# DeltaNet and hash-routed experts on one core: third expert's rows ahead of its weights, and other filler products in a planned order

## Chip, cores and metric

The kernel runs on one core of one Trainium2 chip. The metric is the device time of one execution in microseconds (us), given as the median of several runs. Everything is float32.

## What is computed

The reference has two stages. First, for 4 batches x 8 heads, a recurrence over 768 steps with a 48 x 48 state; then a mixture of 8 experts over the 3072 resulting rows of 384 numbers, where each row goes to exactly one expert, chosen by a hash of its token number.

```python
k_n = k / (norm(k) + 1e-6)
for t in range(S):                      # S = 768, D = 48, B = 4, H = 8
    y[:, :, t] = q[t] @ state
    v_old = state . k_n[t]
    state = state + beta[t] * outer(k_n[t], v[t] - v_old)
x = y.transpose(0, 2, 1, 3).reshape(B * S, H * D)       # 3072 x 384
expert_idx = token_ids * 2654435761 % 8
for e in range(8):
    xe = x[expert_idx == e]
    out[expert_idx == e] = relu(xe @ w1[e]) @ w2[e]      # 384 -> 1024 -> 384
```

## The kernel before

**Recurrence.** Time is cut into 24 chunks of 32 steps, and four chunks make a group. Per group the keys and queries are loaded (SP queue), turned on the tensor engine PE (`turn`, L457) and copied from PSUM to the tile KQ or wide by the scalar engine ACT (L462). Products of keys with keys and with queries follow: `first_gram` (L525) for the first group, `gram` (L483) for the others; ACT and the vector engine DVE copy them out as GK and GQ (L493, L500, L503, L509, and L537, L538 for the first group). `inverse` (L581 to L624) inverts a 32 x 32 triangular matrix per chunk and head on DVE in pairs of operations, a multiply into tmp (L624) and an add into U (L622); `turn_back` (L638) transposes it for PE.

Each chunk then is a chain across engines: PE multiplies the state with keys (L690, L659 into psX) and queries (L659 into psY), ACT makes the residual R (L695), PE solves with the inverse (L709), ACT copies W (L723), PE updates the state (L738 into psS) and finishes the answer (L779 into psY), ACT copies the new state S (L762) and the rows x_sb (L788), and GpSimd (POOL) scatters the rows, sorted by expert, into a DRAM scratch (L794).

**The order is planned, not written.** Every step of that stage is recorded by `task` with an engine, an assumed duration and what it reads and writes. `order` (L286) plays a greedy schedule of these tasks when the program is built and emits each engine's instructions in the planned order; on the chip each engine runs its own list strictly in that order. While it plans, `fill` (L320) looks at each planned idle stretch of PE in front of a task. If the stretch is over FILL_OVER (380 ns) and begins before FILL_UNTIL, it puts products of the identity matrix (emitted at L1192) in front of that task, of 128 to 512 columns each, into a PSUM bank that the plan holds to be unused. Nobody reads these products. How much idle time of one stretch may be filled is capped: at 1100 ns, except in the first 2 us. Each filler also counts two instruction words (`issued += 2`). The planner assumes that instructions are fetched in blocks of 256 words and lets PE's tasks wait for them, so another number of words also shifts planned start times and with them the order of later tasks.

**Experts.** RANKS orders the eight experts as 4, 0, 1, 2, 3, 5, 6, 7. The first is computed inside the planned stage: its products (L1041, L1052, and for the rows of the last chunks L1065 and L1075) are low-priority tasks that take PE's idle time. Its late hidden values, h_late, lie in the row buffer xq0, and L1075 is what reads them last. The other seven come after it as plain code. For each, `gemm1` (L1226) makes 8 hidden blocks of three products each in four PSUM banks in turn; ACT applies the relu to the even blocks (L1229), DVE to the odd ones (L1231). Then comes the second product (L1263, turned back by L1273 and copied by L1248; or L1242), and POOL scatters the rows to the output (L1252). Inside `gemm1` the function `between` starts what later experts need: after block 0 the weights of an expert further on, after block 1 the row fetch of the expert after the next, and after blocks 1, 3 and 5 DVE turns one third of the next expert's rows (L108), in DVE's own list ahead of its later relus.

All these loads are on one queue, SP's, which issues in program order and stops at a load whose buffer isn't free:

- `fetch` (L100, L104): four row loads into xq0 or xq1 and one small load of token numbers. Second, fourth, ... expert by rank use xq1; the third uses xq0.
- `load_w` (L94 four loads of 384 KB, L117 one of 1536 KB): an expert's weights.

At the start of the part that follows the planned stage, L1303 to L1307 issue: rows of the second expert, its weights (`parts`, eight loads at L94 and L125), weights of the third expert, rows of the third expert.

```python
            fetch(RANKS[1])                                                             # 1303
            for part in parts:
                part()
            w_tiles[2] = load_w(expert_at(RANKS[2], mybir.EngineType.SP), w_pool2, nc.sync)
            fetch(RANKS[2])                                                             # 1307
```

Of the kernel before, what the change touches and what calls it, by code (L numbers as in the profile page):

```python
# [20 lines left out]
def kernel(  # L21
# [27 lines left out]
    RANKS = [4, 0, 1, 2, 3, 5, 6, 7]  # L49
# [35 lines left out]
    def value(at, engine, top):  # L85
        return nc.values_load(ov_i[0:1, at:at + 1], engines=[engine], min_val=0, max_val=top)

    def expert_at(rank, engine):
        return value(AT_E + rank, engine, E - 1)

    def w1_parts(e, w1_sb, eng):

        w1 = moe_w1[bass.ds(e, 1)].rearrange("o d f -> (o d) f")
        return [lambda j=j: eng.dma_start(  # L94
            out=w1_sb[C * j:C * j + C],
            in_=w1[QD * j:QD * j + QD].rearrange("(c d) f -> d c f", d=C)) for j in range(4)]

    def load_x(row, blocks, xq, eng):
        rows = x_dram[bass.ds(row, C * blocks)].rearrange("(i t) x -> t i x", t=C)
        return [eng.dma_start(out=xq[C * j:C * j + C, 0:blocks, 0:QD],  # L100
                              in_=rows[:, :, QW * j:QW * j + QD]) for j in range(4)]

    def load_numbers(row, cols, width, to, eng):
        return eng.dma_start(out=to, in_=x_dram[bass.ds(row, cols * width), QD:QD + 1].rearrange(  # L104
            "(c p) x -> p c x", c=cols))
# [5 lines left out]
    def load_w(e, pool, eng):  # L111
        s2 = moe_w2[bass.ds(e, 1)].rearrange("o f d -> (o f) d")
        w1_sb = pool.tile([P, CO, F], F32, name="w1_sb")
        for part in w1_parts(e, w1_sb, eng):
            part()
        w2_sb = pool.tile([P, FO, DIN], F32, name="w2_sb")
        eng.dma_start(out=w2_sb, in_=s2.rearrange("(fo p) d -> p fo d", p=P))  # L117
        return w1_sb, w2_sb
# [40 lines left out]
    with ExitStack() as phase1:  # L159
# [9 lines left out]
        BANK = 512  # L169
        LATE = NU - GC  # L170
        SEED, SPREAD, PATIENCE = 1, 0.0, 0.2
        FILL_OVER, FILL_UNTIL = 380.0, 80000.0

        st = phase1.enter_context(tc.tile_pool(name="st", bufs=1))
        iv_stack = ExitStack()
# [110 lines left out]
        def order():  # L286
# [33 lines left out]
            def fill(i, idle, at):  # L320

                nonlocal issued
                rate = 1.67
                if at < 2000:

                    rate, idle = 3.34, idle - 900
                idle = min(idle, 2750 if at < 2000 else 1100)
                while idle > FILL_OVER and at < FILL_UNTIL:
                    unused = [b for b in range(len(homes)) if banks[b] is not None
                              and banks[b] <= at]  # L330
                    if not unused:
                        break
                    n = min(4, max(1, int((idle - 160) / (rate * P))))
                    fills.setdefault(i, []).append((unused[0], n))
                    issued += 2
                    idle -= n * rate * P
                    at += n * rate * P
# [17 lines left out]
            while len(done) < n:  # L355
                best, can = None, {}
                for e, r in ready.items():
                    can[e] = [(x, i) for x, i in ((when(x, i), i) for x, i in r)
                              if x is not None]
                    if can[e]:  # L360
                        at = max(free[e], min(x for x, _ in can[e]))
                        if best is None or at < best[0]:
                            best = (at, e)
                at, e = best
# [27 lines left out]
                if e == "PE":  # L392
                    fill(pick, s - free[e], free[e])
# [55 lines left out]
        def turn(g, a, b):  # L449
            KQ, src, job = KQs[g % 4], (KTs, QTs)[a][b], new_job(1, early=g < 3)  # L450

            def view():
                return bank(job).rearrange("p (u x) -> p u x", u=HU)

            def go():
                for u in range(HU):
                    nc.tensor.transpose(view()[:, u, :],  # L457
                                        src[:, u].rearrange("p r d -> p (r d)"), ident)

            task("PE", 540, (f"t{a}{b}",), (f"j{job}",), go, words=8, job=(job, 0))  # L460
            task("ACT", 490, (f"j{job}",), (f"KQ{g % 4}{a}{b}",),
                 lambda: nc.scalar.activation(KQ[:, :, a, b, :], view(), ACT.Copy),  # L462
                 job=(job, 0))
# [739 lines left out]
    with tc.tile_pool(name="w_pool2", bufs=2) as w_pool2, \  # L1203
# [18 lines left out]
        def gemm1(w1_sb, xT, h_sb, width, between=None):  # L1222
            for fo in range(FO):
                h_ps = hidden()
                for co in range(CO):
                    nc.tensor.matmul(h_ps[:, :width], lhsT=w1_sb[:, co, fo * P:(fo + 1) * P],  # L1226
                                     rhs=xT[:, co, :width], start=(co == 0), stop=(co == CO - 1))
                if fo % 2 == 0:
                    nc.scalar.activation(h_sb[:, fo, :width], h_ps[:, :width], ACT.Relu)  # L1229
                else:  # L1230
                    nc.vector.tensor_scalar(out=h_sb[:, fo, :width], in0=h_ps[:, :width],  # L1231
                                            scalar1=0.0, scalar2=None, op0=ALU.max)
                if between is not None:
                    between(fo)
# [16 lines left out]
        def send_rows(rows, idx, alone):  # L1251
            scat = nc.gpsimd.indirect_dma_start(  # L1252
                out=out[:, :], out_offset=bass.IndirectOffsetOnAxis(ap=idx, axis=0),
                in_=rows, in_offset=None, bounds_check=N - 1, oob_is_err=False)
            if alone:
                tc.declare_no_dep(scat.ins, group="scatters", reason="disjoint rows")
                tc.add_to_no_dep_group("scatters", scat.ins)
# [10 lines left out]
        def send(oT, e, col):  # L1268

            o_ps = results()  # L1270
            cw = CWS[e]
            for i in range(CO):
                nc.tensor.transpose(o_ps[0:cw, i * P:(i + 1) * P],  # L1273
                                    oT[:, i, col * cw:(col + 1) * cw], ident)
            store(o_ps, col, cw, idx[e][0:cw, col:col + 1], True)
# [4 lines left out]
        def own(e):  # L1280
            return KTS[e], CWS[e], (CAPS[e] + C - 1) // C, xqs[RANKS.index(e) % 2]

        def fetch(e):
            cols, cw, blocks, xq = own(e)
            row = value(AT_ROW + e, mybir.EngineType.SP, N)
            load_x(row, blocks, xq, nc.sync)
            xns[e] = m_i.tile([P, KT], F32, name="numbers")
            load_numbers(row, cols, cw, xns[e][0:cw, 0:cols, None], nc.sync)
# [13 lines left out]
        with tc.manual_schedule():  # L1302
            fetch(RANKS[1])  # L1303
            for part in parts:
                part()
            w_tiles[2] = load_w(expert_at(RANKS[2], mybir.EngineType.SP), w_pool2, nc.sync)
            fetch(RANKS[2])  # L1307
            n_ov = nc.values_load(ov_i[0:1, NOV:NOV + 1], min_val=0, max_val=NOV)
            for c in range(CO):
                turn(RANKS[1], c)  # L1310
            for k in range(SC):
                send_rows(o_first[:, k], idx_i[:, k:k + 1], True)
            send_rows(o_late, idx_i[:, SC:SC + 1], True)
            for i, e in enumerate(RANKS):
                if e == FIRST:
                    continue
                w1_sb, w2_sb = w_tiles.pop(i)
                rest = [e for e in RANKS[i + 1:i + 3]]
                done = RANKS[i - 1] if RANKS[i - 1] in oTs else None

                def between(fo):

                    to = max(3, i + 1)
                    if fo == 0 and to < E and to not in w_tiles:
                        w_tiles[to] = load_w(expert_at(RANKS[to], mybir.EngineType.SP),
                                             w_pool if to == 4 else w_pool2, nc.sync)
                    elif fo == 1 and len(rest) > 1:
                        fetch(rest[1])
                    if fo % 2 and fo // 2 < CO and rest:
                        turn(rest[0], fo // 2)  # L1330
                    if fo % 2 and done is not None:
                        send(oTs[done], done, fo // 2)

                h_sb = m_h.tile([P, FO, CAP], F32, name="h_sb")
                gemm1(w1_sb, xTs.pop(e), h_sb, CAPS[e], between)
                if KTS[e] > CO:
                    oTs[e] = m_t.tile([P, CO, CAP], F32, name="oT")
                    for j in range(CO):
                        gemm2_turned(w2_sb, h_sb, oTs[e], j, CAPS[e])
                else:  # L1340
                    cols, cw, _, _ = own(e)
                    for j in range(cols):
                        gemm2(w2_sb, h_sb, j, cw, idx[e][0:cw, j:j + 1], True)
# [49 lines left out]
```

## Time and profile before

| | |
|---|---|
| median of 3 runs | 505.26 us (505.12 to 509.08) |
| the profiled execution | 498.96 us |
| its span, first to last instruction | 497.4 us |
| mean granted clock of PE | 0.970 |
| PE busy / DVE / ACT / POOL | 92% / 46% / 39% / 14% |
| planned stage, up to the first product of the second expert | 0 to 255.3 us |
| seven further experts on PE | 255.3 to 485.9 us |

A timeline row gives start, duration, engine, line, operation, output and input by the program's names, shapes, how many instructions were merged, and in brackets how long the engine sat idle before it and what ended that. One float32 product is two MATMUL records in the trace. In the table of stages, each engine has its busy time and the number of its instructions; PEclk is the granted clock of PE as a share of full speed.

### The profile page before, as it was taken

Reading aid. Unit: us, or ns where it says so; the run is one execution under the profiler, and the core shown is the slowest. Engines: PE = TensorE matmul, PEld = TensorE weight load, DVE = VectorE, ACT = ScalarE, POOL = GpSimd, SP = SyncE. Lnnn points to the kernel's source line nnn. Section 1 sums busy time; section 2 is a strip of 40 time slices with the busy share of each in tenths; the row PEclk is TensorE's granted clock in tenths of the full one; section 3 lists DMA queues with packets and bytes.
Section 4 is the critical chain, followed back from the end, with each engine's and each line's share of the span. In section 5 each row is a group of like instructions: output and inputs, shape, how many; then the busy total and the mean of one; then the engine's idle time right before and its main releaser. Section 6 shows DMA issues by size and latency. Waiting matters only on the chain. (4 is left out here: it accounts for less than half of the span.)

```text
span 497.4 us, 15828 instructions
## 1 busy us (share of the span) xinstructions
PE 459.2 (92%) x6648; PEld 312.5 (63%) x6648; DVE 228.8 (46%) x720; ACT 191.7 (39%) x443; POOL 71.6 (14%) x106
## 2 busy tenths in 40 slices
PE   8882899999899899899998999999999999999990
PEld 6762677787687777787754555555555565655650
DVE  5799979998998889850102013012021130110100
ACT  4762779988698687441221011011011110100100
POOL 6000101202020022320020012113011022001010
PEclk9996699999999899999999999999999999999996
DMA  9997756679444447523999995645543016401010
GB/s 137 170 154 116 114 112 132 131 151 189 99 101 100 100 112 176 151 72 77 186 271 246 244 222 140 152 129 114 112 151 73 0 39 164 144 7 39 0 31 15
DMA packets 137180, 60.61 MB, mean 122 GB/s; under 512 B 123005, under 2 KB 131825, under 8 KB 137108
## 3 DMA queue, kind: packets, MB, share of 16 engines
q1 hardware_dynamic: 131572, 49.80, 49.6%
q0 software_dynamic: 5344, 9.66, 6.1%
q8 instruction: 53, 0.87, 0.8%
q10 hardware_dynamic: 192, 0.12, 0.2%
q14 instruction: 19, 0.16, 0.1%
HBM read 49.19 MB, written 10.42 MB: 120 GB/s over the span
## 5 line engine op out<-in xcount | busy, mean ns | idle before, releaser
L1263 PE MATMUL bank<-h_sb,w_sb 128*128 128x424 f32 (+1 forms) x192 | 66.4, 506 | 0.0
L624 DVE TENSOR_TENSOR tmp<-U,Ni 128x87 f32<-128x87 f32 (+15 forms) x186 | 62.2, 339 | 3.2
L622 DVE TENSOR_TENSOR U<-U,tmp 128x87 f32<-128x87 f32 (+15 forms) x186 | 61.8, 338 | 2.9
L1252 POOL DMA_INDIRECT out_dram<-o_sb,tokens x25 | 29.3, 1172 | 199.2 <-ACT o_sb L1248 154.2
L1226 PE MATMUL z<-xT,w_sb 128*128 128x424 f32 (+3 forms) x168 | 57.4, 491 | 0.0
L1263 PEld LDWEIGHTS bank<-h_sb,w_sb 128*128 128x128 f32 x192 | 36.2, 190 | 28.4 <-issue 15.6
L794 POOL DMA_INDIRECT x_scratch<-x_sb,slot x24 | 24.8, 1031 | 183.0 <-ACT MT L550 50.5
L1231 DVE TENSOR_SCALAR h_sb<-z 128x424 f32<-128x424 f32 (+3 forms) x14 | 7.9, 562 | 88.5 <-PE z L1226 88.5
L1242 PE MATMUL bank<-w_sb,h_sb 128*121 128x384 f32 (+1 forms) x144 | 46.9, 486 | 0.0
L762 ACT ACTIVATE S<-psS 48x384 f32<-48x384 f32 (+1 forms) x92 | 42.7, 465 | 9.2 <-PE psS L738 7.9
L1226 PEld LDWEIGHTS z<-xT,w_sb 128*128 128x128 f32 x168 | 31.6, 190 | 22.2 <-issue 7.6
L1242 PEld LDWEIGHTS bank<-w_sb,h_sb 128*121 128x121 f32 (+1 forms) x144 | 26.6, 185 | 19.4
L779 PEld LDWEIGHTS psY<-W,MT 64*64 64x64 f32 x768 | 25.5, 138 | 11.1 <-issue 9.6
L1265 ACT COPY oT<-bank 128x424 f32<-128x424 f32 (+1 forms) x8 | 4.0, 499 | 72.9 <-PE bank L1263 72.9
L1226 PE MATMUL psY<-xT,w_sb 128*128 128x424 f32 (+3 forms) x84 | 30.0, 493 | 1.7 <-DVE h_sb L1231 1.7
L1248 ACT COPY o_sb<-bank 106x384 f32<-106x384 f32 (+3 forms) x14 | 6.7, 479 | 64.0 <-PE bank L1242 49.6
L779 PE MATMUL psY<-W,MT 64*64 64x48 f32 x768 | 29.1, 224 | 1.2 <-issue 1.2
L1226 PE MATMUL psX<-xT,w_sb 128*128 128x424 f32 (+3 forms) x84 | 29.9, 492 | 0.0
L738 PE MATMUL psS<-W,K 32*128 32x96 f32 x736 | 26.7, 280 | 2.5 <-ACT W L723 2.2
L738 PEld LDWEIGHTS psS<-W,K 32*128 32x128 f32 x736 | 22.7, 186 | 5.5 <-ACT W L723 3.6
L709 PE MATMUL psX<-R,Tz 64*64 64x48 f32 x672 | 25.2, 223 | 0.4 <-issue 0.2
L550 ACT ACTIVATE Tz<-TU,kmask 128x256 f32<-128x256 f32 x40 | 23.8, 716 | 3.7 <-DVE TU L638 3.7
(205 smaller groups left out, 665.6 us busy)
## 6 DMA issues: line engine op xcount, KB each, us to landing
w_sb<-in_moe_w_dram SPq DMA_DIRECT2D x32, 384.0 KB
w_sb<-in_moe_w_dram SPq DMA_DIRECT2D x6, 1536.0 KB
keys<-in_k_dram SPq DMA_DIRECT2D x24, 192.0 KB
Qt<-in_q_dram SPq DMA_DIRECT2D x24, 192.0 KB
V<-in_v_dram SPq DMA_DIRECT2D x96, 48.0 KB
K<-in_k_dram SPq DMA_DIRECT2D x96, 48.0 KB
wide<-in_moe_w_dram SPq DMA_DIRECT2D x8, 384.0 KB
xq<-x_scratch SPq DMA_DIRECT2D x12, 144.0 KB
```

What stands on the lines that cost most here:

```text
L550: lambda e=e: nc.scalar.activation(out[:, :, e].rearrange(order_of), in_.rearrange(order_of), ACT.Copy, scale=kmask[:, e:e + 1]))
L622: nc.vector.tensor_tensor(U[:, n:, 0:n], U[:, n:, 0:n], t, op=ALU.add)
L624: nc.vector.tensor_tensor(t, U[:, j:n, 0:n].to_broadcast([P, m, n]), Ni[:, j, n:, None].to_broadcast([P, m, n]), op=ALU.mult)
L709: nc.tensor.matmul(pws[i][rows, h], lhsT=Tz[rows, h].rearrange("p e i -> p (e i)"), rhs=R[rows, h], start=(h == (hs.start if split else 0) ...
L738: nc.tensor.matmul(state[0][:, b, 2 * D * u:2 * D * u + 2 * D], lhsT=K4[quarter(b), u].rearrange("p r d -> p (r d)"), rhs=W[quarter(b), 2 ...
L762: copy = nc.scalar.activation(put, get, ACT.Copy)
L779: nc.tensor.matmul(py[rows, h], lhsT=MT[rows, h].rearrange("p e i -> p (e i)"), rhs=W[rows, h], start=(c == 0 and h == 0), stop=True, skip ...
L794: put = nc.gpsimd.indirect_dma_start(out=x_dram[0:N, :], out_offset=bass.IndirectOffsetOnAxis(ap=slot[:, c:c + 1], axis=0), in_=x_sb, in_o ...
L1226: nc.tensor.matmul(h_ps[:, :width], lhsT=w1_sb[:, co, fo * P:(fo + 1) * P], rhs=xT[:, co, :width], start=(co == 0), stop=(co == CO - 1))
L1242: nc.tensor.matmul(o_ps[0:rows, 0:DIN], lhsT=h_sb[:, fo, col * rows:(col + 1) * rows], rhs=w2_sb[:, fo, :], start=(fo == 0), stop=(fo == F ...
L1252: scat = nc.gpsimd.indirect_dma_start(out=out[:, :], out_offset=bass.IndirectOffsetOnAxis(ap=idx, axis=0), in_=rows, in_offset=None, bound ...
L1263: nc.tensor.matmul(oT_ps[:, 0:width], lhsT=w2_sb[:, fo, i * P:(i + 1) * P], rhs=h_sb[:, fo, 0:width], start=(fo == 0), stop=(fo == FO - 1))
```

## The change

Three constants or lines move:

```diff
-        FILL_OVER, FILL_UNTIL = 380.0, 80000.0
+        FILL_OVER, FILL_UNTIL = 380.0, 210000.0
...
-                idle = min(idle, 2750 if at < 2000 else 1100)
+                idle = min(idle, 2750 if at < 2000 else 3000)
                 while idle > FILL_OVER and at < FILL_UNTIL:
...
             for part in parts:
                 part()
+            fetch(RANKS[2])
             w_tiles[2] = load_w(expert_at(RANKS[2], mybir.EngineType.SP), w_pool2, nc.sync)
-            fetch(RANKS[2])
```

Fillers are now placed over the whole planned stage, and one planned idle stretch may be filled up to 3000 ns. The row fetch of the third expert stands ahead of its weights on SP's queue.

In the built program this makes 10 more filler products. PE's list has the following, in order:

| where in PE's list | before, columns | after, columns |
|---|---|---|
| start, three fillers | 512, 256, 256 | the same |
| in `first_gram`, before the last quarter of its products (L525) | 512 | 512, 512, 256 |
| among `gram` of the first group (L483) | 384 | 384 |
| in `gram` of the second group (L483) | 512 | 512, 256 |
| after the solve of chunk 0 (L709) | 512 | 512 |
| after two solves (L709), before `gram` products | none | 384, and 512 |
| between the two halves of a state product (L659) | none | 128 |
| after three solves (L709), before the state update (L738) | none | 256, 256, 256 |
| between the two halves of a state product (L659) | none | 256 |

The order of the other instructions is the same up to about chunk 3 and differs from there on PE, ACT, DVE and SP: `gram` and `turn` products move by a few places against the chunks' own products, with the ACT copies and DVE masks that belong to them, and the loads on SP move alike. No other instruction is added or left out.

## Prediction

> **What bounds the kernel now.** I read first the page's slices, then a table of stages, then timelines of single stages. The slices show PE at 8 or 9 tenths nearly everywhere and its granted clock low in one early stretch only:
>
> ```profile
> PE   8882899999899899899998999999999999999990
> ...
> PEclk9996699999999899999999999999999999999996
> ```
>
> The table of stages says which engine limits which stage (start:end, length, then busy time of PE, PE's weight loads, DVE, ACT, POOL with counts, then PEclk, DMA share, GB/s):
>
> ```profile
> 20.00:30.00 10.00, 8.97 (x337) 6.42 (x317) 9.84 (x45) 6.91 (x22) 0.00 (x0) 1.00 1.07 168
> 40.00:50.00 10.00, 2.88 (x159) 2.24 (x159) 10.00 (x43) 3.94 (x17) 0.00 (x0) 0.52 0.88 129
> 160.00:170.00 10.00, 7.55 (x278) 5.81 (x269) 8.82 (x29) 5.85 (x16) 0.00 (x0) 1.00 0.50 105
> 170.00:180.00 10.00, 9.69 (x247) 8.10 (x251) 8.01 (x28) 7.21 (x18) 2.50 (x4) 0.83 0.38 91
> ```
>
> From 20 to 50 us DVE is full: it inverts the first group, and PE has nothing to do before that is done. From 58 to 207 us PE is busy 139.5 of 149 us and DVE 132.3, so PE sits idle 9.5 us there, in pieces, in a chain that runs over PE, ACT and DVE. From 207 us the first expert fills PE (17.9 of 18 us, then 30 of 30), and the seven others keep it full to 485.9 us, 228.5 of 231. So microseconds come from PE's idle time before 207 us, from a delay of the chain, or from the few stalls behind. A start of the chain that is x later leaves PE idle x longer before its last work, since that work isn't less.
>
> **Part one: rows ahead of weights.** Behind 255 us, the waits of PE show one stall:
>
> ```profile
> 268.10 2.30 PE L1226 MATMUL psX<-xT,w_sb 128*128 128x424 f32 x6
> 272.08 2.40 PE L1226 MATMUL psY<-xT,w_sb 128*128 128x424 f32 x6 [1.68 <-DVE h_sb L1231]
> ```
>
> PE wants to reuse PSUM tile psY, whose relu DVE hasn't run. DVE's timeline says why: it stands in front of a turn whose rows are late.
>
> ```profile
> 270.89 0.65 DVE L108 STREAM_TRANSPOSE xT<-xq 128x448 f32<-128x448 f32 x1 [10.46 <-DMA xq<-x_scratch]
> 271.46 0.56 DVE L1231 TENSOR_SCALAR h_sb<-psY 128x424 f32<-128x424 f32 x1
> ```
>
> SP's timeline has the third expert's weights (243.14, 249.14) ahead of its rows (255.49):
>
> ```profile
> 243.14 5.30 SPq L94 DMA_DIRECT2D w_sb<-in_moe_w_dram  x4
> 249.14 0.39 SPq L117 DMA_DIRECT2D w_sb<-in_moe_w_dram  x1
> 255.49 8.51 SPq L100 DMA_DIRECT2D xq<-x_scratch  x4
> ```
>
> The rows start no earlier after the change: they go into xq0, which L1075 reads up to 255.29. What changes is that SP now stands there from 242.2 with the five weight loads behind it, and the rows meet an empty queue. The second expert's rows did that: issued at 232.80 in 1.89 us, first turn at 238.4, 5.6 us later. So the third's are there at about 255.5 + 5.6 = 261.1. DVE reaches the turn at 260.4 (259.84 + 0.60) and waits 0.7 us. A wait of 10.46 us cost PE 1.68, so one under 8.8 us costs nothing: **-1.7 us**, between 0 and the 2.4 us that the weight loads show for this wait.
>
> The step moved has five DMAs, and the five it goes past start 14.6 us later, at about 257.7. These are 3072 KB; at the 246 GB/s of that slice they need 12.5 us and are there by 271 to 273. The third expert's first product is at 291.39, so 18 us are left. Behind them on SP stand the fourth expert's weights (needed about 326 us) and rows (turned at 296.38). All from 257.7 to those rows is about 7.5 MB, 30 us, so 288, with 8 us left and nearly 9 more before PE would feel it. The cover is thus DMA rate; were it gone, every us by which the weights pass 291.4 is one on PE. POOL's queue is not passed.
>
> **Part two: a longer filler in the first group.** Here a filler stands in front of the last quarter of the first products, three rows of PE and one each of ACT and DVE:
>
> ```profile
> 11.15 1.13 PE L1192 MATMUL z<-ident 128*128 128x512 f32 x2
> 12.20 0.21 PE L525 MATMUL psX<-KQ 48*32 48x32 f32 x1
> ```
>
> ```profile
> 9.96 0.60 ACT L462 ACTIVATE KQ<-bank 128x512 f32<-128x512 f32 x1 [0.87 <-PE bank L457]
> 13.99 1.08 ACT L538 ACTIVATE GK<-psX 128x512 f32<-128x512 f32 x1 [3.43 <-PE psY L525]
> ```
>
> ```profile
> 14.04 1.08 DVE L537 COPY GK<-psY 128x512 f32<-128x512 f32 x1 [2.42 <-PE psY L525]
> ```
>
> The operand of that quarter is ready at 9.96 + 0.60 = 10.56, and the products before it start their last at 11.03. The filler therefore already stands on the path; it is not in idle time. ACT and DVE both wait for these products, and DVE goes from there into the stretch in which it is full until 50 us. The change makes 512 columns into 1280. Rate: L1263 does 24 products of 424 columns in 17.24 us, 1.69 ns a column. 768 x 1.69 = **+1.3 us**. Lower bound 0, if some slack took it in; I find none, since DVE has 10.00 of 10 busy before chunk 0 begins and the chunks follow from that. If the filler's own row is taken (1.05 us for 512), it is 1.6.
>
> The 256 columns more at 26 us (0.43 us) lie in front of products for the second group, whose transpose on DVE starts at 39.55, while ACT has copied them by 32.4. Hidden by 7 us; cost 0, at most 0.43.
>
> **Part three: seven new fillers late.** 384 + 512 + 128 + 4 x 256 = 2048 columns, 3.5 us of PE. Between 0 (all in idle time) and 3.5 (none). The nearest row is the gap in front of the state update, which three of them are put in:
>
> ```profile
> 188.48 1.15 PE L738 MATMUL psS<-W,K 32*128 32x96 f32 x32 [0.59 <-ACT W L723]
> ```
>
> 0.43 fits into 0.59. The two in front of `gram` (0.65, 0.87) fit where PE waits as at 161.80 (1.06), and not where it doesn't; the two inside a state product (0.22, 0.43) may displace. I take **+0.4**.
>
> **What they can win: the clock.** The low clock of 170 to 180 us is this:
>
> ```profile
> 170.14 0.87 PE L659 MATMUL psX<-S,wide 128*32 128x96 f32 x16 [0.60 <-ACT S L762]
> 170.78 1.51 PE L659 MATMUL psY<-S,wide 128*32 128x96 f32 x32
> 172.22 1.72 PE L709 MATMUL psX<-R,Tz 64*64 64x48 f32 x32
> ```
>
> From start to start 0.64, 1.44 and 1.55 us; the same work later takes 0.35, 0.80 and 1.06. So the dip costs 1.4 us, and it follows a stretch in which PE was idle 2.4 of 10 us, the longest gap 1.06. The Trainium skill ("TensorE: Matmul & The Clock Gate", section on why this matters for kernels) speaks against the change: the clock drops after idle gaps over some 3 us. By that rule, no filler of 0.2 to 0.9 us in gaps of 1 us can win anything here, and the sum below is 0.7 higher. The row shows a drop without such a gap, so I give it half: **-0.7**, from 0 to -1.4.
>
> The other low clock, 0.5 from 43 to 57 us, is not touched: no filler is added between 28 and 150 us, where the idle stretch lies.
>
> **The new order.** From chunk 3 on, products change places. No row prices that. What it can reach is DVE's waits from 20 to 207 us, of which those for the `gram` results are 3.4 (behind ACT's copy) and 1.2 us (behind PE). The `gram` rows move forward in PE's and DVE's lists, so part of these 4.6 us may go; as much may be added if DVE's masks now stand ahead of products that aren't ready. Between -4.6 and +4.6; I take a quarter, **-1.2**.
>
> **Sum:** -1.7 + 1.3 + 0 + 0.4 - 0.7 - 1.2 = -1.9 us. On the profiled execution, 498.96 (497.4 of span and 1.6 around it), that is 497.1. The runs' median is 6.3 us above it, at 505.26; what makes that difference isn't in the trace, and I put the same 1.9 on it: **503.4 us**.
>
> **Rivals.**
> - *The fillers and the order pay in full* (0.17): the dip goes, the 4.6 us of waits go, the late fillers are free: -1.7 + 1.3 - 1.4 - 4.6 = -6.4, 498.9. For it: PE has 9.5 us idle to give. Against: DVE is nearly as full, and four of the seven fillers stand where chunks wait on ACT.
> - *Slower: fillers stand in front of products whose operands are there* (0.20). As at 12.20, PE runs in its own order and can't pass them. Place: the first group and the seven late ones. Price: 1.3 + 3.5, against 1.7 won, nothing else: +3.1, 508.4. It decides from the point where more than 0.4 us of the 3.5 is not in idle time.
> - *The change does nothing* (0.13): the stall of 1.68 us goes, the start comes 1.3 us later, and order, clock and late fillers cancel: -0.4, 504.9. Or the weights, 14.6 us later, take the stall over; that needs less than 3.7 MB in 33 us, 112 GB/s, and the slices there show over 220.
> - *Forecast* (0.50): 501.5 to 505.5 by itself.
>
> **How the numbers follow.** The range takes the forecast and the greater part of both sides: 499.5 (the good rival without its last half us) to 508.5 (the slow one). About 1% is what a measurement of this kernel tells from no change: 500.2 and 510.3. Below 500.2 lies most of the first rival: 0.14. Above 510.3 lies the slow rival with a bad order on top: 0.06. The rest, 0.80, is within.
>
> **What would show it.** Rows: no PE wait at L1226 for DVE's relu, and third-expert turns from about 261. First group: L525's last quarter starting near 13.5 in place of 12.20, GK copies at 15.3, the first L638 at 49.4 in place of 48.15. Clock: 1.00 in all rows between 60 and 255. Late fillers: L1192 rows with an idle gap or none before the row that follows. If the first L638 isn't later, part two is wrong; if the first L1226 is over 2 us from 255.3 either way, the order or the late fillers are mis-sized; if PE waits for w_sb at L1226 or L1263, part one is.

## The result, and the profile after

| | before | after |
|---|---|---|
| median, 18 runs each | 506.74 us (502.77 to 510.01) | 503.41 us (502.5 to 504.91) |
| ratio, 95% interval | | 0.9941 (0.992 to 0.9961) |
| profiled execution, its span | 498.96, 497.4 us | 502.5, 500.9 us |
| granted clock of PE, mean | 0.970 | 0.975 |
| first product of the second expert | 255.29 us | 260.83 us |

0.59% of 506.74 us is 3.0 us gained, with the whole interval below 1; 1.9 were forecast. That is less than the 1% by which the prediction told a change from none. A ratio leaves out executions more than 1.5% above the fastest of their kernel; in the last group of runs below that takes 18 of 66 from the kernel before, and plain medians there give the kernels in the new order 0.989 to 0.991. The two profiled executions stand the other way round, 497.4 against 500.9 us. That cannot be the change: on the chips of the experiments the same two kernels have medians near 499.5 and 495.9 us. So durations and waits are read from the trace of after here, and starts from pairs taken together.

The page's slices of the changed kernel, with PE's busy tenths and its clock:

```profile
PE   8983999999999999999999999999999999999990
...
PEclk9986799999999999999999999999999999999996
```

The 8 at the place of 160 to 175 us is gone. The table of stages (columns as before), for three of the same stretches:

```profile
40.00:50.00 10.00, 2.11 (x136) 1.86 (x136) 10.00 (x42) 3.86 (x16) 0.00 (x0) 0.62 0.64 107
...
160.00:170.00 10.00, 9.47 (x334) 6.72 (x337) 8.15 (x27) 6.35 (x16) 0.00 (x0) 1.00 0.59 135
170.00:180.00 10.00, 9.81 (x261) 7.59 (x258) 8.88 (x31) 8.83 (x21) 2.53 (x4) 1.00 0.34 76
```

DVE is full up to 50 us as before (9.90 us of the ten from 20 us). From 160 to 180 us PE was idle 2.4 of 10 us and then had a mean clock of 0.83; now it is idle 0.5 and the clock is 1.00. Three of the fillers (0.91, 1.12 and 0.49 us of rows) lie in that stretch or at its edge, so busy is not the same as useful.

Rows of the third expert, PE's timeline and DVE's:

```profile
265.10 2.30 PE L1226 MATMUL psX<-xT,w_sb 128*128 128x424 f32 x6
267.24 2.30 PE L1226 MATMUL psY<-xT,w_sb 128*128 128x424 f32 x6
```

```profile
267.35 0.65 DVE L108 STREAM_TRANSPOSE xT<-xq 128x448 f32<-128x448 f32 x1 [1.37 <-DMA xq<-x_scratch]
269.57 0.60 DVE L1231 TENSOR_SCALAR h_sb<-psY 128x424 f32<-128x424 f32 x1 [1.58 <-PE psY L1226]
```

And the loads on SP's queue:

```profile
261.03 2.14 SPq L100 DMA_DIRECT2D xq<-x_scratch  x4
...
265.10 3.41 SPq L94 DMA_DIRECT2D w_sb<-in_moe_w_dram  x4
```

No bracket is left on PE: DVE waited 1.37 us for the rows in place of 10.46 and then waited for PE, not PE for it. The rows came 267.35 - 261.03 = 6.3 us after their issue (5.6 forecast). Behind 262 us PE has no wait in the table of waits, so the weights that start later are hidden.

The first group, on PE and on DVE:

```profile
10.69 2.42 PE L1192 MATMUL z<-ident 128*128 128x512 f32 x6
13.04 0.21 PE L525 MATMUL psX<-KQ 48*32 48x32 f32 x1
```

```profile
14.31 1.09 DVE L537 COPY GK<-psY 128x512 f32<-128x512 f32 x1 [2.69 <-PE psY L525]
```

The filler takes 2.42 us where it took 1.13, and the last quarter starts at 13.04. DVE's copy is at 14.31 (14.04 before), although the operand was there 0.45 us earlier (10.11 against 10.56). DVE's first L638 starts at 48.23, against 48.15 before and 49.4 forecast. And one of the late fillers, ahead of the state update:

```profile
197.24 0.70 PE L1192 MATMUL z<-ident 128*128 128x256 f32 x2
197.89 1.15 PE L738 MATMUL psS<-W,K 32*128 32x96 f32 x32
```

### The profile page after: what moved, and what is told of

Same layout as the page of the kernel before. It is cut to its first block, busy times and chain, and to the rows that moved or that the text cites. A ratio compares the mean times of both kernels' runs of the same rounds, so it can differ in the third digit from the quotient of the medians.

```text
span 500.9 us, 15876 instructions
## 1 busy us (share of the span) xinstructions
PE 468.7 (94%) x6668; PEld 317.2 (63%) x6668; DVE 229.5 (46%) x720; ACT 192.0 (38%) x443; POOL 70.6 (14%) x106
## 5 line engine op out<-in xcount | busy, mean ns | idle before, releaser
L1226 PE MATMUL z<-xT,w_sb 128*128 128x424 f32 (+3 forms) x168 | 57.4, 491 | 0.0
L794 POOL DMA_INDIRECT x_scratch<-x_sb,slot x24 | 24.4, 1015 | 189.5 <-ACT MT L550 82.0
L762 ACT ACTIVATE S<-psS 48x384 f32<-48x384 f32 (+1 forms) x92 | 42.7, 464 | 10.9 <-PE psS L738 9.6
L1226 PEld LDWEIGHTS z<-xT,w_sb 128*128 128x128 f32 x168 | 31.6, 190 | 22.2 <-issue 7.6
L1226 PE MATMUL psX<-xT,w_sb 128*128 128x424 f32 (+3 forms) x84 | 29.9, 492 | 0.0
L1226 PE MATMUL psY<-xT,w_sb 128*128 128x424 f32 (+3 forms) x84 | 29.9, 491 | 0.0
L709 PE MATMUL psX<-R,Tz 64*64 64x48 f32 x672 | 26.4, 221 | 2.5 <-issue 1.9
L779 PE MATMUL psY<-W,MT 64*64 64x48 f32 x768 | 27.8, 220 | 0.1
L738 PE MATMUL psS<-W,K 32*128 32x96 f32 x736 | 27.2, 280 | 0.4 <-ACT W L723 0.2
L709 PEld LDWEIGHTS psX<-R,Tz 64*64 64x64 f32 x672 | 22.6, 134 | 7.6 <-issue 4.7
L1231 DVE TENSOR_SCALAR h_sb<-psY 128x424 f32<-128x424 f32 (+3 forms) x14 | 7.9, 565 | 40.7 <-PE psY L1226 40.7
```

The source lines that it names most:

```text
L709: nc.tensor.matmul(pws[i][rows, h], lhsT=Tz[rows, h].rearrange("p e i -> p (e i)"), rhs=R[rows, h], start=(h == (hs.start if split else 0) ...
L738: nc.tensor.matmul(state[0][:, b, 2 * D * u:2 * D * u + 2 * D], lhsT=K4[quarter(b), u].rearrange("p r d -> p (r d)"), rhs=W[quarter(b), 2 ...
L762: copy = nc.scalar.activation(put, get, ACT.Copy)
L779: nc.tensor.matmul(py[rows, h], lhsT=MT[rows, h].rearrange("p e i -> p (e i)"), rhs=W[rows, h], start=(c == 0 and h == 0), stop=True, skip ...
L794: put = nc.gpsimd.indirect_dma_start(out=x_dram[0:N, :], out_offset=bass.IndirectOffsetOnAxis(ap=slot[:, c:c + 1], axis=0), in_=x_sb, in_o ...
```

## Three theories, and the runs

R: the gain is the stall behind 255 us that the earlier rows take away. F: it is the filler products, by keeping PE's clock up or by standing in its idle time. P: it is the planned order, which differs from chunk 3 on because each filler counts two words in the plan; the filler products themselves are beside the point.

Times are compared with the kernel before on the same chip: eight kernels in two groups on one chip (before: medians 498.79 and 499.68 us), the last four on another (500.12). All of them but the kernel before and "fills without the rows" have the rows ahead. Kernels of which it is said that fillers are not emitted leave out products that nobody reads, so their output is that of the reference.

**Rows alone, twice.** The kernel before with this edit:

```diff
+            fetch(RANKS[2])
             w_tiles[2] = load_w(expert_at(RANKS[2], mybir.EngineType.SP), w_pool2, nc.sync)
-            fetch(RANKS[2])
```

> The kernel before with only the row fetch moved ahead of the weights. Theory R (the stall at the third expert is the whole gain, the fillers and the new order cancel): 3 us faster than before, ratio 0.994, spread of its runs as wide as before's (7 us). Theory F (the fillers or the order they bring give part of the gain and take the spread away): 1.7 to 2.0 us faster, ratio 0.996 to 0.9966, spread still 7 us. Both: no PE wait for DVE's relu at L1226; third expert's turns about 5.6 us after its fetch is issued.

> The rows ahead alone, a second time, since 0.9994 with an interval of 0.0028 either way does not tell zero from the 1.7 us that its trace shows. Theory of the forecast (the stall of 1.7 us goes): 0.9966. Theory that the stall is 1 us or less in most executions: 0.998. Rival (the removed stall is given back, nothing gained): 1.000. Both runs taken together have an interval of about 0.002.

Measured: 0.9994 (0.9966 to 1.0022) and 0.9983 (0.9955 to 1.0011). The mean, 0.9989, is -0.6 us, give or take about 1. Both traces have no stall left, and from the first L1226 to the end they take 240.2 us, where the kernel before takes 242.1 in one trace and 241.4 in a second. So a trace shows 1.2 to 2 us; the times confirm a sign at most. R does not carry 3 us.

**Fills without the rows.** The changed kernel with the two lines put back in their old order.

> The changed kernel with the row fetch put back behind the weights: only the fillers and the order that follows from them. Theory R: ratio 1.000 (within 0.2%), the PE stall of 1.7 us at L1226 still there. Theory F: 1.3 to 1.6 us faster than before, ratio 0.997, and runs within 2.5 us of each other as with the whole change.

Measured: 0.9957 (0.9932 to 0.9981). Most of the gain is there without the rows. Here the stall at L1226 is only 0.2 us: it depends on when that stage starts against the rows, and is not a fixed 1.68.

**The order without the fillers, twice.** The changed kernel, with its plan, but the ten new fillers are not emitted:

```diff
-                for b, n in fills.get(i, ()):
+                for b, n in fills.get(i, ())[:{106: 1, 275: 1}.get(i, 9)] if start[i] < 80000 else ():
```

> The changed kernel with its plan and so its order, but without the ten new filler products (they count in the plan and are not issued; nobody reads them, so no result changes). If the fillers themselves win (clock): slower than the whole change by 1 to 2 us, ratio to before 0.997 to 0.998, with dips of the granted clock between 150 and 260 us. If they only cost PE time: faster than the whole change by up to 3 us, ratio 0.988. If order alone makes the difference: like the whole change, 0.994.

> The new order alone, a second time, beside the six-word kernel and the late fillers on the same chip. Theory P: 0.992 again, within 0.003, equal to the six-word kernel and to the late fillers within 0.002. If it comes back at 0.996 or more, its first result was the luck of the executions, and the order is worth less than 2 us.

Measured: 0.992 (0.9889 to 0.9951) and, on the other chip, 0.9943 (0.9915 to 0.9971). The whole gain is there with not one new product.

**The fillers without the order.** The kernel before with its order kept exactly and the rows ahead; the new fillers are emitted but count no words in the plan. By the old order's gaps these are 13, three more than in the change.

```diff
-                idle = min(idle, 2750 if at < 2000 else 1100)
+                counted, idle = min(idle, 2750 if at < 2000 else 1100), min(idle, 2750 if at < 2000 else 3000)
...
-                    issued += 2
+                    issued += 2 if counted > FILL_OVER and at < 80000 else 0
```

> Row fetch ahead, fillers by the new constants, but the extra ones aren't counted as instruction words, so every other instruction stands as before: thirteen more filler products in before's order. Against the rows alone it shows the fillers by themselves. If the clock matters: 1 to 2 us faster than the rows alone and a narrow spread. If a filler in the first group costs what the prediction said: 1.3 us slower than the rows alone. If neither: the same within 0.2%.

Measured: 1.0012 (0.9984 to 1.0039). F fails on both sides: the order without fillers earns, the fillers without the order do not. The clock in this one trace is low at another place than before:

```profile
130.00:140.00 10.00, 9.37 (x197) 6.56 (x198) 8.00 (x35) 5.30 (x13) 1.58 (x2) 0.83 0.50 120
...
170.00:180.00 10.00, 9.99 (x282) 8.04 (x284) 8.73 (x31) 8.41 (x21) 2.50 (x4) 1.00 0.45 103
```

From 160 to 170 us it is 1.00 as well. Two fillers stand at 166.1 and 167.1 us here, and the dip that before had behind them is gone. Whether they took it away one trace can't say; the times show no gain from it.

**Both kernels again, side by side on one chip.**

> The kernel before once more, unchanged, on the same chip as the runs sent with it, for a trace that can be laid beside theirs. If the stall of 1.7 us at L1226 is the rule in before's executions, it is there again; if the rows alone didn't show in the times because the stall comes and goes, it is gone or smaller.

> The whole change, unchanged, beside before on one chip. Theory R: ratio 0.994 and most of it behind the first L1226. Theory P (the plan's new order is the gain: leaving the ten fillers out gave 0.992, the rows alone 0.9994): ratio 0.993 to 0.996, first L1226 about 1 to 2 us earlier than in the trace of before sent with it, fillers costing about 1 us against the order without them.

Measured: 0.9929 (0.9904 to 0.9955) for the changed kernel; the kernel before was run once here, 501.58 us. The trace of before now shows what the first trace of it did not. Its table of stages, and PE's timeline at the place:

```profile
160.00:170.00 10.00, 7.90 (x231) 7.00 (x231) 7.66 (x24) 4.18 (x11) 0.00 (x0) 0.63 0.34 79
170.00:180.00 10.00, 10.00 (x200) 7.86 (x203) 6.16 (x24) 6.76 (x17) 1.48 (x3) 0.69 0.29 64
```

```profile
162.10 0.28 PE L659 MATMUL psX<-S,wide 128*32 128x96 f32 x3 [2.26 <-issue]
```

In the middle of a state product PE stops for 2.26 us, and no wait for another engine is in the trace ("issue"). What it waits for can be seen all the same. PE's instructions come by DMA on queue 8, in 53 packets of 16 KB (0.87 MB) for 13,296 products and weight loads, about 251 each; the page lists them as

```profile
q8 instruction: 53, 0.87, 0.8%
```

One of these packets starts at 159.60 us and takes 1.22 us, and PE goes on 1.28 us after its end. All 14 traces together have 71 stops of PE with "issue" of more than 0.5 us. Every one ends 1.2 to 1.8 us after the end of such a packet, where 13% of times drawn at random would lie. So PE waits there for instructions that come late. In the first trace of before, the same packet starts at 157.25 us and PE does not stop at this place; why it starts later here is not shown.

The 0.63 and 0.69 that follow are means. In the stretches that the traces record, the clock is only ever 1.00 or 0.50, and here it is 0.50 for 13.65 us:

```profile
162.62:176.27 13.65, 13.65 (x323) 11.31 (x314) 8.92 (x29) 7.55 (x18) 1.40 (x2) 0.50 0.33 72
```

In the first trace of before, the 0.83 is one stretch of 3.41 us at 0.50, from 170.12.

**Without the filler in the first group.** The edit of the order alone, with `106: 0` in place of `106: 1`: no product stands in front of the last quarter.

> The order of the changed kernel, none of the ten new fillers, and also no filler in the first group (before has 512 columns there; nobody reads them). If that filler stands on the path, as the prediction said: the first L638 starts 0.5 to 1.0 us earlier than with 512 columns and the time falls by as much, ratio 0.990. If the products behind it are held by something else: the same as with it, 0.992.

Measured: 0.9948 (0.9915 to 0.998), no better than the order alone. PE's timeline says why:

```profile
12.68 0.19 PE L525 MATMUL psY<-KQ 48*32 48x32 f32 x1 [1.84 <-issue]
```

Only the first 7 of the last quarter's 64 MATMUL records start earlier, from 10.58 us. Then PE waits until 12.68 for instructions, whose packet ended at 10.97. In all nine traces with 512 columns PE stops at nearly the same place, after 5 of the 64, for 0.26 to 0.66 us; with 1280 it does not stop. From the start of the KQ copy on ACT that this quarter needs (9.96 us in the first trace of before) to DVE's GK copy it is 4.3 us with no filler, 3.9 to 4.4 (median 4.12) in the nine with 512 columns, and 4.8 in the four with 1280.

**Words alone.** The kernel before with rows ahead, its old constants for the fillers, and the plan's counter set higher at the start. First eight words, then six, whose edit is shown without the move of the rows:

```diff
-            issued, begun, have = 60, [], 900.0
+            issued, begun, have = 66, [], 900.0
```

> Before with the rows ahead and one number changed: the plan counts 68 instruction words at the start in place of 60; constants for the fillers as before. Theory P says that the order follows from a count and may turn out better or worse: this order is another one, and by itself it moves the first L1226 by one to several us either way, with no filler involved. Theory F (the new fillers carry the gain): within 0.2% of the rows alone, 0.9994.

> The kernel before with rows ahead of weights and one number changed: the plan begins with 66 counted words in place of 60. No filler is added or made longer; the planned order becomes that of the changed kernel but for eight places on PE. Theory P (the order is what earns): 0.991 to 0.994, as the order alone (0.992). Theory F (fillers earn): 0.998 to 1.001, as the rows alone (0.9994). A value of 0.996 would say that those eight places, or the spread, weigh as much as the order.

Measured: eight words (68) 0.9942 (0.9917 to 0.9968), six 0.9951 (0.9926 to 0.9976). Six give the changed kernel's order but for eight places in PE's list, and no filler is added. Eight give a third order, and in it the plan places two fillers more (512 columns at 34.4 us, 256 at 75.7) and makes one shorter. With six words, a number that emits nothing thus earns what the change earns. The table of stages with six words, at the place of the stop in the old order:

```profile
160.00:170.00 10.00, 9.06 (x345) 7.21 (x338) 8.78 (x30) 7.83 (x20) 0.00 (x0) 1.00 0.57 114
170.00:180.00 10.00, 9.71 (x286) 7.81 (x280) 9.18 (x29) 7.98 (x20) 3.80 (x6) 1.00 0.45 105
```

ACT is busy 15.8 us of these 20 where it was 10.9 in the trace with the stop, and the clock stays at 1.00, with no filler anywhere near.

**Late fillers alone.** The changed kernel with `{106: 1, 275: 1}` as the only cut, so the first groups have their old 512 columns and the seven late fillers stay.

> The changed kernel with 512 columns in front of the last quarter of the first group's products, as before the change, and 512 in the second group; the seven late fillers, the new order and the rows ahead stay. Left out against the changed kernel: 1024 columns of products that nobody reads. Theory P (the order earns the time, late fillers cost and win nothing, the first-group filler costs 0.6 us): ratio 0.991 to 0.993, as the order alone (0.992) and slightly under the changed kernel (0.9929); first state-to-answer product stage starts with its first turned inverse near 47.8 us, as with 512 columns before. Theory F (late fillers win by themselves, by keeping the clock): 0.988 to 0.990 and a smaller spread than the order alone, 1.5 us or less. Rival (late fillers cost their 3.5 us): 0.996 or more.

Measured: 0.9947 (0.9925 to 0.997), beside 0.9943 for the order alone in the same group. Late fillers neither cost nor win what could be measured, and the spread of the executions that the ratios count is not smaller: 1.5 us of standard deviation against 1.2.

## Where the time came from

POOL's timeline gives the start of each chunk's scatter (L794). Sorted by the order that a kernel has, in us:

| order | chunk 12 to 13 | chunk 13 to the last | last scatter |
|---|---|---|---|
| old: before, twice | 15.4, 18.9 | 54.1, 54.1 | 225.4, 228.7 |
| old: rows alone, twice | 15.4, 18.7 | 54.2, 53.8 | 225.5, 230.0 |
| old: fillers uncounted | 15.8 | 53.4 | 226.7 |
| new, none or 512 early, no late fillers: order alone twice, six words | 14.6, 15.0, 14.6 | 52.8, 53.6, 54.2 | 223.8, 224.9, 224.3 |
| new, with late fillers: late only, fills without rows, the changed kernel again | 15.7, 15.9, 16.2 | 52.5, 52.5, 52.8 | 223.2, 223.6, 224.4 |
| new, no first-group filler | 16.6 | 55.8 | 228.1 |
| new, the changed kernel in the first comparison | 16.0 | 56.8 | 231.0 |
| a third order: eight words | 12.1 | 56.1 | 228.3 |

In the old order the last scatter is at 227.2 us on average, in the six traces of the two middle rows at 224.0: 3.2 us, of which 1.5 lie between chunks 12 and 13, at 156 to 175 us. Those 1.5 come from the two traces with the stop of 2.26 us (18.9 and 18.7); the other three of the old order have 15.4 to 15.8, no more than the rows with late fillers. The rest is spread, 0.8 and 0.9 us ahead of it and behind. The last three rows are late, though their kernels are as fast in their times as the others; with both late traces in the new order the 3.2 us become 1.8. Each trace is one execution, so these differences show where time can go and not how much it is on average.

Less waiting for instructions in total is not what the new order brings. From 60 us to the first L1226, PE's waits for issue are 2.4 to 5.1 us in the five traces of the old order, and 2.9 to 4.0 in the four of the new that have no new fillers. What differs more is the time at a clock of 0.50 in that stretch: 3.4, 13.7, 3.4, 13.7 and 3.4 us in the old order; in the new, none in six of eight traces, 3.4 us at 128 us in one of the order alone, and 10.2 us without the first-group filler. But the kernel with eight words has 10.2 us of it too, from 120 us on, in a trace that is 3.4 us above its median.

Over all their executions the mean clock is 0.967 to 0.970 in the old order and 0.971 to 0.973 in the new, again without the kernel that has no first-group filler, which has 0.966. Among the kernel before's own executions the time falls by 290 to 370 us per whole unit of clock, so the 0.004 between the two groups are some 1.2 to 1.5 us (an estimate): up to half of the gain. Which comes first, less waiting or the better clock, is not shown. Nor is the new order a guarantee: without the first-group filler, PE waited 0.92 us for issue at 164 us and 1.09 at 195, and the mean clock of the ten us around fell to 0.77 and 0.83.

## Why the prediction came near

The total was right in sign and near in size (-1.9 forecast, -3.0 measured), the terms were less so, and they made up for each other by luck. That 503.4 was forecast and 503.41 measured is luck too: the forecast stood on a median of 505.26 from 3 runs, where 18 give 506.74, and from there -1.9 leads to 504.8.

- **Rows ahead, -1.7.** Right in mechanism, over-sized. The stall went, the turns came when forecast, the weights stayed hidden. But 1.68 us was one execution's: it is 1.0 in a second trace of before and 0.2 in the new order. Times gave -0.6, give or take 1; in the new order the swap has little left to take away.
- **First-group filler, +1.3.** The filler row grew by 2.42 - 1.13 = 1.29 us, as worked out, but DVE's copy comes only 4.81 - 4.12 = 0.69 us later, and the first L638, the sign that was named, about 0.5 us later from the same KQ copy (38.7 us against 38.2) in place of 1.3. The step that failed is "I find no slack": the products behind the filler were short of instructions, and took 1.7 to 2.1 us from their first to DVE's copy behind 512 columns but 1.28 behind 1280. With no filler at all PE waits 1.84 us for them. The 256 columns in the second group were not measured by themselves.
- **Late fillers, +0.4.** About 0: 0.9947 with them, 0.9943 without. The traces with them are about 1.2 us slower between chunks 12 and 13 and about 0.9 faster behind.
- **The clock, -0.7, given to the fillers.** The dip went, as the clock check of the prediction asked for, but it is no measure of the gain. It is gone with six counted words and no new filler, and it is gone from that place with fillers in the old order, which earn nothing. What the times show belongs to the order: the mean clock is 0.004 higher with it, some 1.2 to 1.5 us (the estimate above). On the rule of the Trainium skill ("TensorE: Matmul & The Clock Gate", section "Why this matters for your kernels"), that the clock falls after idle gaps over some 3 us: the longest gaps here, 1.06 and 2.26 us, are shorter, and the clock still fell to 0.50, for 3.4 and 13.7 us. The measurement stands against the figure. Between 60 us and the first L1226, every stretch at 0.50 in the 14 traces is a multiple of 3.41 us long. Counted in windows of that length, the ten drops there come after windows in which PE was busy 34 to 75%, and none after a busier one; 13 windows of 67 to 75% had no drop behind them.
- **The new order, -1.2 (-4.6 to +4.6).** The term that decided: with the 0.6 us of the rows taken off, the order alone gives some -2 to -3.5 us. Right sign, wrong place: I looked for it in DVE's waits for `gram` results. They are 4.6 and 6.1 us in the two traces of before, 6.7 and 5.2 in those of the changed kernel and 4.1 with six words, so they say nothing clear of where the time went. What the traces show of it is PE's stop for instructions and the time at half clock, which the trace of before held in part only; the rest of the gain has no place yet.

Of the rivals, "slower by fillers in front of ready products" fell with 0.9947 and 1.0012; "pays in full" had the dip right and the DVE waits wrong. Of the signs named, the first L1226 within 2 us of 255.3 failed in the first trace of after (260.83) and held in its repeat (254.23), while the repeat of before has 258.51: single traces could not carry that sign.

Left open: how this order changes when PE's instructions come, why the clock falls again without the first-group filler, and why the trace of after in the first comparison is 6.6 us longer in its span than its repeat, with the same clock (0.975): its chunks take some 0.4 us more each from the fifth on. A version that beats the changed kernel was not found. The order alone (0.992, 0.9943) lies beside it (0.9941, 0.9929), within the intervals.

## What to carry to other kernels

When an edit feeds a planner, test the plan's new order with the edit's own instructions taken out, and the instructions with the old order kept: here the order was all of the gain that could be measured, and a counter moved by six gave the same. A stall read from one trace is a sample, so look at a second trace before it goes into a sum. A product put in front of ready work costs less than its length where the engine is waiting for its own instructions (0.69 us of 1.29 here).

## What was not expected of the hardware

- Executions of one program differ by 7 to 15 us in a group, and the time follows the granted clock: the kernel before, in the runs of the experiments, has a standard deviation of 2.2 to 2.7 us and a correlation of -0.7 to -0.8 between time and mean clock.
- PE can stop for 2.26 us in the middle of a row of equal products with only "issue" as the reason, in two of five traces of the old order, at the same product; the packet with its next instructions ends 1.3 us before it goes on.
- The clock falls to 0.50 for 13.65 us after one stop of 2.26 us, with PE busy all through the low stretch.
- The same kernel has a median of 506.74 us in one comparison, and of 498.79 to 500.12 in the others.
